# Causal attention with two routed expert layers on one core: score tiles paired 3 with 0 and 2 with 1, and another order of the products in odd and even steps

## The chip, the cores and the metric

The program runs on one NeuronCore of a Trainium2 chip. TensorE (PE in the profile, with its weight loads as PEld) multiplies matrices into PSUM, which has eight banks; VectorE (DVE) and ScalarE (ACT) read PSUM and work on SBUF; GpSimd (POOL) and SyncE (SP) issue transfers, and GpSimd does some elementwise work. The metric is the device time of one execution in microseconds, median of several runs.

## The reference, cut to what matters

```
attn (4 batches, 12 heads, 448 rows, 64 wide):
  scores = q @ k.T / 8, masked above the diagonal
  p = exp(scores - max(scores)); p = p / (sum(p) + 1e-9); x = p @ v
x -> 1792 tokens x 768
moe : skip = x @ w_skip; e = argmax(x @ w_gate); g = softmax at e
      where skip > 0:  x = x + g * (relu(x @ w1[e]) @ w2[e])
moe2: e = argmax(xn @ en.T / tau), xn and en with unit norm; g = softmax at e
      x = g * (relu(x @ w1[e]) @ w2[e])
```

## The kernel before

The first quarter of the program (up to 235 us) is attention and the first router; the rest sends tokens to 8 experts twice. The change is all in attention.

Attention is one loop over the 48 heads, `i` = 0 to 47. It runs under `manual_schedule`, so on each engine the instructions stand in the order in which the code emits them, and each engine takes them in that order; what one engine needs of another it waits for by semaphore. Step `i` works on several heads at once:

- scores of head `i-1`: the 448 rows are four chunks of 112, and by causality chunk `c` has (c+1)*112 columns. `scores` (L303) writes one product for each chunk, in the order 2, 3, 1, 0. q and k of a head are 64 deep and lie twice in SBUF, on partitions 0 to 63 and on 64 to 127, so that a product uses one half of the array's rows: `r` picks the half.
- `stage_a` (L310): for a chunk, one VectorE instruction scales, masks and takes the row maximum (L318, `st` and `mn`), and one ScalarE instruction takes exp and the row sum (L321, `pr`).
- `turn` (L550), head `i-2`: ten transposes of `pr` by TensorE in three groups (L331, tiles `tp`), each group copied to SBUF (L333, `pt`): the first and third by VectorE, the second by ScalarE.
- for pairs of heads: in an even step `stage_v` (L336) multiplies the turned weights by v for heads `i-4` and `i-3` (16 matmul rows of the trace, tile `av`), ScalarE copies it (L347, `xb`); in the odd step that follows, `turn_v` (L349) transposes `xb` (L353, `tv`), `norm_v` (L356) divides by the row sums on VectorE (L359 to L361, tile `x`), `put_x` sends x to DRAM, and `router_turn` (L370) transposes x (L373, `rt`), which ScalarE copies (L376, `xs`); in the next even step `router_pair` (L378) multiplies it by the router's weights (L386) and VectorE adds it up (L391, `ls`).
- when a batch of 12 heads is through, `route` (L401) hands single pieces to the following steps through the list `later`: `logits` (L393, in steps 17, 29 and 41), `rank` (L454, steps 19, 31 and 43; its sum `rks` L476), one-hot lists on GpSimd, and `enter` (L521, `tk`; steps 24, 27, 36 and 39).

In an odd step from 5 on TensorE has, in order: scores, ten transposes, the router's four transposes. In an even step: scores, values, router's products, ten transposes, and at its end the four transposes of `turn_v` for the odd step that follows. In the odd steps 7 to 17 ScalarE also casts 128x1024 of a later layer's weights (L637).

PSUM: tile `s3` has a bank; chunks 2 and 0 share the tile `s20` in one bank; chunk 1, the router's products `lt` and the logits share the tile `bank`; `tp`, `tv`, `rt`, `rk` and `tk` rotate through four banks; `av` has one. A reader or writer of a tile waits for the last other user of the whole tile, whichever columns it used.

Of the kernel before, what the change touches and what calls it, by code (L numbers as in the profile page):

```python
# [7 lines left out]
F32 = mybir.dt.float32  # L8
# [10 lines left out]
B, H, S, D = 4, 12, 448, 64  # L19
CP = 112  # L20
NCH = S // CP
DM = H * D
DF = 1024
NE = 8
# [21 lines left out]
def moe_attention_kernel(tc, qk, vv, w_r, emb, tau, w11, w12, w21, w22, out):  # L46
# [25 lines left out]
    with ExitStack() as top:  # L72
# [148 lines left out]
        with ExitStack() as ctx:  # L221
# [34 lines left out]
            ern, en = inv_norm(sm, ess, NE, "en")  # L256

            def embed_squares():
                esq = wk.tile([NE, DM], F32, tag="pt", name="esq")
                nc.scalar.activation(esq, es, AF.Square, accum_out=ess)  # L260

            def embed():
                pe = ps.tile([P, 4 * CP], F32, tag="tp", name="pe", bufs=4)
                for k in range(KC):
                    nc.tensor.transpose(
                        pe[:, k * 8 : k * 8 + 8], es[:, k * P : (k + 1) * P], ident[:NE, :NE])
                nc.vector.tensor_copy(wr[:, :, 8:16], pe[:, 0:48].rearrange("p (k e) -> p k e", e=8))
# [8 lines left out]
                    small.pop(0)()  # L276


            bank = ps.tile([P, 4 * P], F32, tag="s1", name="bank")
            lt, lg_room = bank[:, 2 * CP : 3 * CP], bank[:CP, 3 * CP : 3 * CP + NCH * NLG]  # L280

            def busy_here(n):
                if n:
# [10 lines left out]
            def score_tiles():  # L294
                return dict(
                    st=wk.tile([CP, 10 * CP], F32, tag="st", name="st"),
                    mn=wk.tile([CP, NCH], F32, tag="mn", name="mn"),
                    pr=wk.tile([CP, 10 * CP], F32, tag="pr", name="pr"),
                    s3=ps.tile([CP, S], F32, tag="s3", name="s3"),
                    s20=ps.tile([CP, S], F32, tag="s20", name="s20"),  # L300
                    s1=bank[:CP, 0 : 2 * CP])

            def scores(src, a, c):  # L303

                n, r = (c + 1) * CP, 64 * (1 - c % 2)
                a[c] = (a["s20"][:, 3 * CP :], a["s1"], a["s20"][:, 0 : 3 * CP], a["s3"])[c]
                nc.tensor.matmul(a[c], src[r : r + 64, c * CP : (c + 1) * CP], src[r : r + 64, S : S + n],  # L307
                                 start=True, stop=True)

# [14 lines left out]
            def turn_p(pr, pt, i):  # L324

                nb = 4 if i < 2 else 2
                tp = ps.tile([CP, 4 * CP], F32, tag="tp", name="tp", bufs=4)
                for u in range(nb):
                    c, j = BLOCKS[4 * i + u]
                    o = (OFF[c] + j) * CP  # L330
                    nc.tensor.transpose(tp[:, u * CP : (u + 1) * CP], pr[:, o : o + CP], ident[:CP, :CP])  # L331
                dst = pt[:, 4 * i * CP : (4 * i + nb) * CP]
                (nc.scalar.copy if i == 1 else nc.vector.tensor_copy)(dst, tp[:, : nb * CP])  # L333

            def stage_v(g):

                b, hp = divmod(g, H // 2)
                av = ps.tile([P, S], F32, tag="av", name="av")
                for j in range(NCH):
                    o = BLOCKS.index((j, j)) * CP  # L340
                    for u in range(2):
                        nc.tensor.matmul(av[u * D : (u + 1) * D, j * CP :], v_t[b][:, j, 2 * hp + u, :],  # L342
                                         pts[2 * g + u][:, o : o + (NCH - j) * CP],
                                         start=(j == 0), stop=(j == NCH - 1))
                del pts[2 * g], pts[2 * g + 1]
                xb = wk.tile([P, S], F32, tag="xb", name="xb", bufs=1)
                return lambda: nc.scalar.copy(xb, av), xb  # L347

            def turn_v(xb):  # L349

                tv = ps.tile([CP, NCH, P], F32, tag="tp", name="tv", bufs=4)
                for t in range(NCH):
                    nc.tensor.transpose(tv[:, t, :], xb[:, t * CP : (t + 1) * CP], ident)  # L353
                return tv

            def norm_v(g, tv):  # L356
                b, hp = divmod(g, H // 2)
                rs = sums.pop(g)
                nc.vector.tensor_scalar(rs, rs, 1e-9, None, op0=ALU.add)  # L359
                nc.vector.reciprocal(rs, rs)  # L360
                nc.vector.tensor_tensor(  # L361
                    x_t[b][:, :, hp * P : (hp + 1) * P].rearrange("p t (u d) -> p t u d", u=2),
                    tv.rearrange("p t (u d) -> p t u d", u=2),
                    rs.unsqueeze(3).to_broadcast([CP, NCH, 2, D]), op=ALU.mult)
# [2 lines left out]

                return b == B - 1 and k == KC - 1

            def router_turn(b, k):  # L370
                rt = ps.tile([P, 4 * CP], F32, tag="tp", name="rt", bufs=4)
                for t in range(NCH):
                    nc.tensor.transpose(  # L373
                        rt[:, t * CP : (t + 1) * CP], x_t[b][:, t, k * P : (k + 1) * P], ident[:CP, :CP])
                xs = wk.tile([P, S], F32, tag="xs", name="xs")
                return lambda: nc.scalar.copy(xs, rt), (b, k, xs)  # L376
# [24 lines left out]
            def route(b):  # L401
# [51 lines left out]

                def rank():  # L454
                    oh, some = k["oh"], k["some"]
                    rk = ps.tile([P, 4 * CP], F32, tag="tp", name="rk", bufs=4)
                    wd = NCH * 16
                    o16 = oh.rearrange("p t m e -> p t (m e)")
                    r16 = run[:CP].rearrange("p m e -> p (m e)")
# [60 lines left out]

                def enter(m):  # L521
                    roh, voh = k["made"][m]
                    tk = ps.tile([P, NCOL], F32, tag="tp", name="tk", bufs=4)
                    for t in range(NCH):
                        nc.tensor.matmul(tk, roh[:, t, :], voh[:, t, :], start=(t == 0), stop=(t == NCH - 1))
                    if fast:
                        first_index(0, tk)
                    nc.vector.tensor_tensor(tok[m], tok[m], tk, op=ALU.add)
                    while k["fill"]:
                        fill()  # L530
# [17 lines left out]
                        lambda: both(enters[0], q1), q2, q3, enters[1]]  # L548

            def turn(i):  # L550
                pts[i] = wk.tile([CP, 10 * CP], F32, tag="pt", name="pt")
                for u in range(3):
                    turn_p(prs[i], pts[i], u)

            def put_x(g):
                b, hp = divmod(g, H // 2)
                if hp % 2 == 1:
                    c0, c1 = (hp - 1) * P, (hp + 1) * P
                    for xx in (x1, x2):
                        xd = xx[b * S : (b + 1) * S, :].rearrange("(t p) f -> p t f", p=CP)  # L560
                        nc.sync.dma_start(xd[:, :, c0:c1], x_t[b][:, :, c0:c1])
# [11 lines left out]
            spl, prs, pts, sums = {}, {}, {}, {}  # L573
            with tc.manual_schedule():
                busy_here(12)
                exps = []
                for i in range(n):
                    b, h = heads[i]
                    if h == 0:
# [13 lines left out]
                        early_low(EARLY[i])  # L593
                    even = i % 2 == 0
                    if not even and i >= 5:
                        norm_v(i // 2 - 2, turn_v(xb))
                        put_x(i // 2 - 2)
                    if i >= 1:
                        sc = score_tiles()
                        prs[i - 1] = sc["pr"]  # L600
                        for c in (2, 3, 1, 0):
                            scores(spl[i - 1], sc, c)
                        exps = [stage_a(i - 1, sc, c) for c in (2, 3, 1)]
                        exps.pop(0)()
                        little()
                    little()
                    ended = None
                    if even and i >= 4:
                        copy_v, xb = stage_v(i // 2 - 2)
                    add = None  # L610
                    if even and i >= 6:
                        add = router_pair(*pair)
                        ended = pair[0] if pair[1] == KC - 1 else None
                    while exps:
                        exps.pop(0)()
                    if even and i >= 4:
                        copy_v()
                    if i >= 1:
                        stage_a(i - 1, sc, 0)()
                        little()  # L620
                    if add is not None:
                        add()
                    if i == 0:
                        embed_squares()
                    little()
# [5 lines left out]
                    if not even and i >= 5:  # L631
                        copy_x, pair = router_turn(*divmod(i // 2 - 2, H // 2))
                        copy_x()
                    if i == 3:
                        embed()
                    if i + 1 in EARLY:
# [16 lines left out]
                    exps.pop(0)()  # L653
                add()
                turn(n - 2)
                norm_v(n // 2 - 2, turn_v(xb))
                later.pop(0)()
                turn(n - 1)
                copy_x, pair = router_turn(B - 1, KC - 2)
                later.pop(0)()  # L660
                copy_x()
                copy_v, xb = stage_v(n // 2 - 1)
# [544 lines left out]
```

## Time and profile before

| | |
|---|---|
| median of 3 runs | 901.4 us (897.3 to 902.94) |
| profiled execution | 902.78 us, span of the trace 901.1 us |
| PE busy | 824.0 us (91%) |
| DVE, ACT, POOL busy | 554.4 (62%), 474.8 (53%), 135.2 us (15%) |
| mean granted TensorE clock | 0.978 of full speed |
| steps 45 and 46, one pair of heads | 8.39 us, PE 8.09 of it |

Times below are microseconds from the start of the span. A step is counted from the first score product on TensorE to the next step's. The trace groups matmuls of one line and tile that follow each other; a float32 product shows as two matmul rows (two passes).

### The profile page before, as it was taken

What the parts mean: (1) busy time and instruction counts of PE and PEld (TensorE: products, weight loads), DVE (VectorE), ACT (ScalarE), POOL (GpSimd) and SP (SyncE); (2) the same over time, 40 slices, a digit from 0 to 9 for tenths busy, and PEclk for the clock granted to TensorE, in tenths of its full rate; (3) what the DMA queues carried; (4) which work ended last, traced back from release to release, by engine and by line L of the source; (5) the groups of instructions that cost most, each with busy time, mean ns of one, the idle gap of its engine ahead of it and who ended that gap; (6) DMA issues with size and microseconds to landing.
All of it is one profiled execution on the core that took longest, in us unless ns stands there. A gap on an engine that the chain in (4) does not pass through costs nothing. (4 is left out here: it accounts for less than half of the span.)

```text
span 901.1 us, 14898 instructions
## 1 busy us (share of the span) xinstructions
PE 824.0 (91%) x4960; PEld 686.5 (76%) x4960; DVE 554.4 (62%) x1641; ACT 474.8 (53%) x1013; POOL 135.2 (15%) x150
## 2 busy tenths in 40 slices
PE   7998989989797899899999879899999998999994
PEld 5665766666487788788899748789889887889884
DVE  5767767776566688378833476665283268574343
ACT  5777666666455466166612336454272256463252
POOL 1132404013201111011010021011111011110100
PEclk9999999999899899999999999999999999999998
DMA  8979565563636487267710354580451086361000
GB/s 243 315 271 299 165 185 165 167 206 139 202 140 258 175 300 286 72 232 300 299 45 28 145 198 159 197 332 21 149 211 51 19 313 267 133 238 41 37 1 18
DMA packets 59032, 158.22 MB, mean 176 GB/s; under 512 B 13013, under 2 KB 23765, under 8 KB 58448
## 3 DMA queue, kind: packets, MB, share of 16 engines
q1 hardware_dynamic: 52816, 139.33, 43.4%
q0 software_dynamic: 6080, 17.29, 5.4%
q8 instruction: 59, 0.97, 0.5%
q14 instruction: 77, 0.63, 0.2%
HBM read 146.45 MB, written 22.92 MB: 188 GB/s over the span
## 5 line engine op out<-in xcount | busy, mean ns | idle before, releaser
L789 PE MATMUL p<-hi,ht 128*128 128x384 f32 x960 | 241.8, 353 | 8.5 <-DVE ht L773 4.6
L740 DVE TENSOR_TENSOR lo<-raw,hi 128x768 fp32r<-128x768 f32 (+1 forms) x218 | 220.6, 1062 | 8.0 <-ACT hi L736 4.5
L781 PE MATMUL p<-hi,xt 128*128 128x512 f32 x720 | 183.3, 403 | 8.0 <-PEq L1088 3.3
L736 ACT CAST hi<-raw 128x768 fp32r<-128x768 f32 (+1 forms) x218 | 187.3, 923 | 0.6 <-DMA raw<-in_w 0.6
L789 PEld LDWEIGHTS p<-hi,ht 128*128 128x128 f32 x960 | 167.8, 191 | 14.7 <-DVE ht L773 10.6
L781 PEld LDWEIGHTS p<-hi,xt 128*128 128x128 f32 x720 | 140.4, 198 | 37.4 <-ACTq L1088 5.1
L321 ACT ACTIVATE pr<-st,mn 112x336 f32<-112x336 f32 x192 | 99.5, 520 | 60.4 <-DVE mn L318 60.4
L789 PE MATMUL p<-lo,ht 128*128 128x384 f32 x480 | 124.3, 340 | 0.4 <-issue 0.4
L773 DVE SCALAR_TENSOR_TENSOR ht<-tp,ht 128x512 fp32r<-128x512 f32 x60 | 41.4, 689 | 115.3 <-ACT ht L772 106.6
L781 PE MATMUL p<-lo,xt 128*128 128x512 f32 x360 | 96.2, 402 | 0.0
L940 ACT COPY hs<-p 128x512 f32<-128x512 f32 x60 | 34.8, 580 | 106.0 <-PE p L781 67.0
L789 PEld LDWEIGHTS p<-lo,ht 128*128 128x128 f32 x480 | 88.7, 191 | 0.5 <-issue 0.5
L760 ACT CAST xt<-tp 128x384 fp32r<-128x384 f32 (+2 forms) x62 | 30.4, 492 | 109.5 <-PE tp L754 108.8
L761 DVE TENSOR_TENSOR xt<-tp,xt 128x384 fp32r<-128x384 f32 (+2 forms) x62 | 33.3, 544 | 84.5 <-ACT xt L760 81.6
L318 DVE CUSTOM_DVE_ANT_0 st<-s,mask 112x336 f32<-112x336 f32 x144 | 63.5, 465 | 29.4 <-PE s L307 17.8
L781 PEld LDWEIGHTS p<-lo,xt 128*128 128x128 f32 x360 | 67.8, 195 | 11.4
L772 ACT ACTIVATE ht<-tp 128x512 fp32r<-128x512 f32 x60 | 36.0, 600 | 55.1 <-PE tp L798 49.4
L331 PE MATMUL tp<-ident,pr 112*112 112x112 f32 x480 | 57.3, 267 | 0.0
L307 PE MATMUL s<-qk 64*112 64x112 f32 (+2 forms) x288 | 49.6, 450 | 7.1 <-DVE mn L318 7.1
L331 PEld LDWEIGHTS tp<-ident,pr 112*112 112x112 f32 x480 | 47.1, 136 | 8.6 <-issue 7.8
L818 POOL DMA_INDIRECT out<-py,pidx x18 | 19.7, 1093 | 207.7 <-ACT hi L736 75.5
L342 PE MATMUL av<-pt,v 112*64 112x448 f32 (+3 forms) x384 | 50.6, 405 | 0.0
(201 smaller groups left out, 908.3 us busy)
## 6 DMA issues: line engine op xcount, KB each, us to landing
raw<-in_w SPq DMA_DIRECT2D x96, 512.0 KB
raw<-in_w SPq DMA_DIRECT2D x128, 384.0 KB
qk<-in_qk SPq DMA_DIRECT2D x23, 896.0 KB
x<-x SPq DMA_DIRECT2D x24, 448.0 KB
v<-in_vv SPq DMA_DIRECT2D x4, 1344.0 KB
qk<-in_qk SPq DMA_DIRECT2D x2, 448.0 KB
g_n<-x,L POOLq DMA_INDIRECT x23, 4.4
out<-py,pidx POOLq DMA_INDIRECT x18, 3.4
```

Source lines behind the costliest of these rows:

```text
L307: nc.tensor.matmul(a[c], src[r : r + 64, c * CP : (c + 1) * CP], src[r : r + 64, S : S + n], start=True, stop=True)
L318: nc.vector.tensor_tensor_reduce(out=so, in0=a[c], in1=mask[:, S - n : S], scale=-0.125, scalar=3.0e38, op0=ALU.add, op1=ALU.min, accum_ou ...
L321: return lambda: nc.scalar.activation(a["pr"][:, OFF[c] * CP : OFF[c] * CP + n], so, AF.Exp, bias=mn, scale=-1.0, accum_out=rs)
L331: nc.tensor.transpose(tp[:, u * CP : (u + 1) * CP], pr[:, o : o + CP], ident[:CP, :CP])
L342: nc.tensor.matmul(av[u * D : (u + 1) * D, j * CP :], v_t[b][:, j, 2 * hp + u, :], pts[2 * g + u][:, o : o + (NCH - j) * CP], start=(j == ...
L736: copy(hi, raw)
L740: eng.tensor_tensor(lo, raw, hi.bitcast(F32), op=ALU.subtract)
L772: nc.scalar.activation(hi, src, AF.Relu)
L773: nc.vector.scalar_tensor_tensor(lo, src, 0.0, hi.bitcast(F32), op0=ALU.max, op1=ALU.subtract)
L781: nc.tensor.matmul(p1[u], xt[:, k, :, j], r[:, u * 512 : (u + 1) * 512], start=(k == 0 and j == 0 and not low), stop=(k == KC - 1 and low))
L789: mm = nc.tensor.matmul(p2[u], l, r[:, u * (DM // 2) : (u + 1) * (DM // 2)], start=(f == 0 and j == 0), stop=(f == FC - 1 and j == len(ter ...
L940: nc.scalar.copy(hs[:, u * 512 : (u + 1) * 512], p1[u])
```

## The change

- Score tiles: chunks 0 and 3 now take one half of the array's rows, 1 and 2 the other (before: 1 and 3, 0 and 2). Each of the four has a PSUM tile of its own; the router's products and the logits now share the tile `bank` with chunk 0.
- An odd step is now: VectorE's adding of the router's products and ScalarE's copy of the values first, then scores, maxima of chunks 2 and 3, `turn_v` and `norm_v`, maxima of chunks 1 and 0, `turn`, `router_turn`.
- An even step is now: scores, all four maxima, `turn`, then the router's products, and the values last.
- The rotating `tp` tiles are three instead of four; `tv` and `rt` share the bank of `av`; `pt` has three buffers.

```diff
-            bank = ps.tile([P, 4 * P], F32, tag="s1", name="bank")
-            lt, lg_room = bank[:, 2 * CP : 3 * CP], bank[:CP, 3 * CP : 3 * CP + NCH * NLG]
+            bank = ps.tile([P, 4 * P], F32, tag="s0", name="bank")
+            lt, lg_room = bank[:, CP : 2 * CP], bank[:CP, 2 * CP : 2 * CP + NCH * NLG]
...
-                n, r = (c + 1) * CP, 64 * (1 - c % 2)
-                a[c] = (a["s20"][:, 3 * CP :], a["s1"], a["s20"][:, 0 : 3 * CP], a["s3"])[c]
+                n, r = (c + 1) * CP, (0, 64, 64, 0)[c]
+                a[c] = (a["s0"], a["s1"], a["s2"], a["s3"])[c]
...
-                av = ps.tile([P, S], F32, tag="av", name="av")
+                av = turned_room("av")[:, 0:S]
...
+            def turned_room(tag):
+
+                return ps.tile([P, 4 * P], F32, tag=tag, name="turned", bufs=3 if tag == "tp" else 1)
+
+            def turn_v(xb, tag="av"):
+
+                tv = turned_room(tag)[:CP].rearrange("p (t n) -> p t n", t=NCH)
...
                     if not even and i >= 5:
-                        norm_v(i // 2 - 2, turn_v(xb))
-                        put_x(i // 2 - 2)
+                        copy_v()
+                        if add is not None:
+                            add()
                     if i >= 1:
...
-                        exps = [stage_a(i - 1, sc, c) for c in (2, 3, 1)]
-                        exps.pop(0)()
+                        exps = [stage_a(i - 1, sc, c) for c in (2, 3)]
                         little()
                     little()
-                    ended = None
-                    if even and i >= 4:
-                        copy_v, xb = stage_v(i // 2 - 2)
-                    add = None
-                    if even and i >= 6:
-                        add = router_pair(*pair)
-                        ended = pair[0] if pair[1] == KC - 1 else None
+                    if not even and i >= 5:
+                        norm_v(i // 2 - 2, turn_v(xb))
+                        put_x(i // 2 - 2)
+                    if i >= 1:
+                        exps += [stage_a(i - 1, sc, c) for c in (1, 0)]
                     while exps:
                         exps.pop(0)()
...
                     if not even and i >= 5:
                         copy_x, pair = router_turn(*divmod(i // 2 - 2, H // 2))
                         copy_x()
+                    ended, add = None, None
+                    if even and i >= 6:
+                        add = router_pair(*pair)
+                        ended = pair[0] if pair[1] == KC - 1 else None
+                    if even and i >= 4:
+                        copy_v, xb = stage_v(i // 2 - 2)
```

The order of instructions, first VectorE in an odd step (`rs` and `x` are `norm_v`, `s_…` and `bank` the score tiles; `pt` is a copy of `turn`). Before:

```order
L359 TENSOR_SCALAR rs<-rs 112x8
L360 RECIPROCAL rs<-rs 112x8 [waits DVE_49]
L361 TENSOR_TENSOR x_123<-tv,rs 112x4x128 [waits DVE_49,PE_49]
L318 ISA st,mn<-s_605,mask 112x336 [waits PE_49,Activation_49]
L318 ISA mn 112x1
L318 ISA st,mn<-s_604,mask 112x448
L318 ISA mn 112x1
L318 ISA st,mn<-bank,mask 112x224
L318 ISA mn 112x1
L318 ISA st,mn<-s_605,mask 112x112
L318 ISA mn 112x1
```

The same step of the changed kernel:

```order
L396 TENSOR_TENSOR ls<-ls,bank 128x112 [waits PE_49]
L319 ISA st,mn<-s_605,mask 112x336 [waits PE_49,Activation_49]
L319 ISA mn 112x1
L319 ISA st,mn<-s_604,mask 112x448 [waits PE_49]
L319 ISA mn 112x1
L364 TENSOR_SCALAR rs<-rs 112x8
L365 RECIPROCAL rs<-rs 112x8 [waits DVE_49]
L366 TENSOR_TENSOR x_123<-turned,rs 112x4x128 [waits DVE_49,PE_49]
L319 ISA st,mn<-s_606,mask 112x224
L319 ISA mn 112x1
L319 ISA st,mn<-bank,mask 112x112
L319 ISA mn 112x1
```

`norm_v` moved from ahead of the four maxima to between the second and the third, and the maxima of chunks 2 and 3 have each a wait of its own.

TensorE in the odd step of the changed kernel, with the four transposes of `turn_v` (L358) after the scores and the router's (L378) last, up to the scores of the even step; the wait of L378 is for `x`:

```order
L308 MATMUL s_605<-qk_435 112x336 [waits DMAHW5_49]
L308 MATMUL s_604<-qk_435 112x448
L308 MATMUL s_606<-qk_435 112x224
L308 MATMUL bank<-qk_435 112x112 [waits DVE_49]
L358 MATMUL turned<-ident,xb 112x128 [waits Activation_49]
L358 MATMUL turned<-ident,xb 112x128 x3
L332 MATMUL tp<-ident,pr 112x112 x10
L378 MATMUL turned<-ident,x_123 128x112 [waits DVE_49]
L378 MATMUL turned<-ident,x_123 128x112 x3
L308 MATMUL s_661<-qk_435 112x336
```

Before, L353 (`turn_v`) stood at the end of the even step, ahead of the odd step's scores, and the scores of the even step waited for VectorE.

TensorE in the even step, from the router's products on. Before:

```order
L386 MATMUL bank<-xs,wr 32x112 [waits DVE_49,Activation_49]
L386 MATMUL bank<-xs,wr 32x112 x3
L331 MATMUL tp<-ident,pr 112x112 [waits PE_49]
L331 MATMUL tp<-ident,pr 112x112 x3
L331 MATMUL tp<-ident,pr 112x112 [waits PE_49]
L331 MATMUL tp<-ident,pr 112x112 x5
L353 MATMUL tv<-ident,xb 112x128 [waits Activation_49]
L353 MATMUL tv<-ident,xb 112x128 x3
```

The changed kernel:

```order
L391 MATMUL bank<-xs,wr 32x112 [waits DVE_49,Activation_49]
L391 MATMUL bank<-xs,wr 32x112 x3
L343 MATMUL turned<-pt,v_121 64x448 [waits PE_49]
L343 MATMUL turned<-pt,v_121 64x448
L343 MATMUL turned<-pt,v_121 64x336 x2
L343 MATMUL turned<-pt,v_121 64x224 x2
L343 MATMUL turned<-pt,v_121 64x112 x2
```

The values (L342, now L343) moved from ahead of the router's products to behind them. In the changed kernel the wait of L391 for VectorE is for the maximum of chunk 0, which lies in the same tile; before, it was for that of chunk 1.

## Rows read from the trace of the kernel before

**Rows 1.** Steps 45 and 46 together: us, busy us of each engine.
```profile
sum 8.39, PE 8.09 PEld 5.71 DVE 6.12 ACT 6.11 POOL 6.58; mean PE 4.04 PEld 2.85 DVE 3.06 ACT 3.06 POOL 3.29
```

**Rows 2.** Timeline of TensorE, steps 45 and 46: start, us, line, out<-in.
```profile
203.81 1.01 PE L307 MATMUL s<-qk 64*112 64x336 f32 x6
...
206.99 1.01 PE L307 MATMUL s<-qk 64*112 64x336 f32 x6 [0.30 <-DVE mn L318]
207.84 0.54 PE L307 MATMUL bank<-qk 64*112 64x224 f32 x2
208.31 2.11 PE L342 MATMUL av<-pt,v 112*64 112x448 f32 x16
210.34 0.40 PE L386 MATMUL bank<-xs,wr 128*32 128x112 f32 x8
210.67 1.17 PE L331 MATMUL tp<-ident,pr 112*112 112x112 f32 x10
211.68 0.60 PE L353 MATMUL tv<-ident,xb 128*112 128x128 f32 x4
212.21 0.63 PE L307 MATMUL s<-qk 64*112 64x336 f32 x2
```

**Rows 3.** Timeline of VectorE, steps 45 and 46.
```profile
203.81 0.16 DVE L359 TENSOR_SCALAR rs<-rs 112x8 f32<-112x8 f32 x1
...
204.30 0.69 DVE L361 TENSOR_TENSOR x<-tv,rs 112x512 f32<-112x512 f32 x1
...
206.85 0.08 DVE L318 DVE_READ_ACCUMULATOR2_ANT mn<- 112x1 f32 x1
...
208.54 0.51 DVE L318 CUSTOM_DVE_ANT_0 st<-s,mask 112x336 f32<-112x336 f32 x1 [0.77 <-ACT pt L333]
...
208.97 0.62 DVE L318 CUSTOM_DVE_ANT_0 st<-s,mask 112x448 f32<-112x448 f32 x1
...
209.51 0.38 DVE L318 CUSTOM_DVE_ANT_0 st<-bank,mask 112x224 f32<-112x224 f32 x1
...
209.83 0.27 DVE L318 CUSTOM_DVE_ANT_0 st<-s,mask 112x112 f32<-112x112 f32 x1
210.02 0.08 DVE L318 DVE_READ_ACCUMULATOR2_ANT mn<- 112x1 f32 x1
```

**Rows 4.** Timeline of ScalarE, from step 45's third exp to its last copy.
```profile
207.14 0.46 ACT L321 ACTIVATE pr<-st,mn 112x224 f32<-112x224 f32 x1
...
208.39 0.52 ACT L376 COPY xs<-rt 128x448 f32<-128x448 f32 x1
```

**Rows 5.** Steps 12, 17, 19, 27, 29, 30, 41: us, busy us (instructions), granted clock, DMA.
```profile
50.58:56.19 5.61, 5.44 (x46) 3.47 (x47) 3.80 (x15) 5.61 (x19) 2.36 (x1) 1.00 0.93 271
73.76:78.42 4.66, 3.07 (x25) 2.44 (x24) 3.28 (x13) 2.73 (x10) 0.00 (x0) 1.00 1.05 357
83.64:87.82 4.18, 3.28 (x28) 2.50 (x27) 3.80 (x18) 2.19 (x10) 0.00 (x0) 1.00 1.01 366
118.41:122.29 3.88, 3.18 (x27) 2.40 (x26) 3.38 (x15) 1.84 (x8) 0.00 (x0) 1.00 0.48 131
127.52:132.88 5.36, 3.77 (x26) 3.00 (x25) 4.12 (x18) 2.75 (x10) 0.00 (x0) 0.86 0.87 245
132.88:139.04 6.16, 6.16 (x48) 4.15 (x47) 3.62 (x20) 3.72 (x12) 0.00 (x0) 0.84 0.43 150
182.91:189.00 6.09, 4.50 (x26) 3.73 (x25) 4.12 (x18) 3.03 (x10) 0.00 (x0) 0.75 0.23 87
```

**Rows 6.** Timeline of TensorE: start of step 2's scores, and of step 17's logits.
```profile
9.10 1.01 PE L307 MATMUL s<-qk 64*112 64x336 f32 x6 [2.04 <-DVE mn L318]
...
76.74 0.41 PE L396 MATMUL bank<-ident,ls 128*112 128x68 f32 x2 [1.59 <-DVE mn L318]
```

**Rows 7.** Timeline of VectorE, step 19: first and last instruction of the rank.
```profile
86.57 0.26 DVE L469 TENSOR_REDUCE some<-oh 112x16 bf16<-112x64 bf16 x1
...
87.02 0.22 DVE L476 COPY rks<-rk 112x64 f32<-112x64 f32 x1
```

More of the change, by code (lines that the diff above doesn't have):

```diff
@@ L258, in embed_squares @@
             def embed_squares():
-                esq = wk.tile([NE, DM], F32, tag="pt", name="esq")
+                esq = wk.tile([NE, DM], F32, tag="pt", name="esq", bufs=3)
                 nc.scalar.activation(esq, es, AF.Square, accum_out=ess)
             def embed():
-                pe = ps.tile([P, 4 * CP], F32, tag="tp", name="pe", bufs=4)
+                pe = ps.tile([P, 4 * CP], F32, tag="tp", name="pe", bufs=3)
                 for k in range(KC):
@@ L299, in score_tiles @@
                     s3=ps.tile([CP, S], F32, tag="s3", name="s3"),
-                    s20=ps.tile([CP, S], F32, tag="s20", name="s20"),
-                    s1=bank[:CP, 0 : 2 * CP])
+                    s2=ps.tile([CP, 3 * CP], F32, tag="s2", name="s2"),
+                    s1=ps.tile([CP, 2 * CP], F32, tag="s1", name="s1"),
+                    s0=bank[:CP, 0:CP])
             def scores(src, a, c):
-                n, r = (c + 1) * CP, 64 * (1 - c % 2)
-                a[c] = (a["s20"][:, 3 * CP :], a["s1"], a["s20"][:, 0 : 3 * CP], a["s3"])[c]
+                n, r = (c + 1) * CP, (0, 64, 64, 0)[c]
+                a[c] = (a["s0"], a["s1"], a["s2"], a["s3"])[c]
                 nc.tensor.matmul(a[c], src[r : r + 64, c * CP : (c + 1) * CP], src[r : r + 64, S : S + n],
@@ L326, in turn_p @@
                 nb = 4 if i < 2 else 2
-                tp = ps.tile([CP, 4 * CP], F32, tag="tp", name="tp", bufs=4)
+                tp = ps.tile([CP, 4 * CP], F32, tag="tp", name="tp", bufs=3)
                 for u in range(nb):
@@ L347, in stage_v @@
                 return lambda: nc.scalar.copy(xb, av), xb
-            def turn_v(xb):
-                tv = ps.tile([CP, NCH, P], F32, tag="tp", name="tv", bufs=4)
+            def turned_room(tag):
+                return ps.tile([P, 4 * P], F32, tag=tag, name="turned", bufs=3 if tag == "tp" else 1)
+            def turn_v(xb, tag="av"):
+                tv = turned_room(tag)[:CP].rearrange("p (t n) -> p t n", t=NCH)
                 for t in range(NCH):
@@ L368, in direct, with router_turn @@
                 return b == B - 1 and k == KC - 1
-            def router_turn(b, k):
-                rt = ps.tile([P, 4 * CP], F32, tag="tp", name="rt", bufs=4)
+            def router_turn(b, k, tag="av"):
+                rt = turned_room(tag)[:, 0 : 4 * CP]
                 for t in range(NCH):
@@ L455, in rank @@
                     oh, some = k["oh"], k["some"]
-                    rk = ps.tile([P, 4 * CP], F32, tag="tp", name="rk", bufs=4)
+                    rk = ps.tile([P, 4 * CP], F32, tag="tp", name="rk", bufs=3)
                     wd = NCH * 16
@@ L522, in enter @@
                     roh, voh = k["made"][m]
-                    tk = ps.tile([P, NCOL], F32, tag="tp", name="tk", bufs=4)
+                    tk = ps.tile([P, NCOL], F32, tag="tp", name="tk", bufs=3)
                     for t in range(NCH):
@@ L550, in turn @@
             def turn(i):
-                pts[i] = wk.tile([CP, 10 * CP], F32, tag="pt", name="pt")
+                pts[i] = wk.tile([CP, 10 * CP], F32, tag="pt", name="pt", bufs=3)
                 for u in range(3):
@@ L575, in moe_attention_kernel @@
                 busy_here(12)
-                exps = []
+                exps, add = [], None
                 for i in range(n):
@@ L602, in moe_attention_kernel @@
                             scores(spl[i - 1], sc, c)
-                        exps = [stage_a(i - 1, sc, c) for c in (2, 3, 1)]
-                        exps.pop(0)()
+                        exps = [stage_a(i - 1, sc, c) for c in (2, 3)]
                         little()
                     little()
-                    ended = None
-                    if even and i >= 4:
-                        copy_v, xb = stage_v(i // 2 - 2)
-                    add = None
-                    if even and i >= 6:
-                        add = router_pair(*pair)
-                        ended = pair[0] if pair[1] == KC - 1 else None
+                    if not even and i >= 5:
[3 more added lines that the diff above has]
+                        exps += [stage_a(i - 1, sc, c) for c in (1, 0)]
                     while exps:
                         exps.pop(0)()
-                    if even and i >= 4:
-                        copy_v()
                     if i >= 1:
-                        stage_a(i - 1, sc, 0)()
                         little()
-                    if add is not None:
-                        add()
                     if i == 0:
@@ L655, in moe_attention_kernel @@
                 turn(n - 2)
-                norm_v(n // 2 - 2, turn_v(xb))
+                norm_v(n // 2 - 2, turn_v(xb, "tp"))
                 later.pop(0)()
                 turn(n - 1)
-                copy_x, pair = router_turn(B - 1, KC - 2)
+                copy_x, pair = router_turn(B - 1, KC - 2, "tp")
                 later.pop(0)()
```

## The prediction, made before the changed kernel ran

> **What bounds the kernel now.** I read first what a pair of steps costs and who is busy in it, then TensorE's timeline of the pair, then VectorE's beside it. The pair of steps 45 and 46 takes 8.39 us and TensorE is busy for 8.09 of it, VectorE for 6.12 and ScalarE for 6.11 [rows 1]. So TensorE's own order sets the pace, with one wait in the pair: the scores of the even step wait for VectorE's last maximum, idle 0.30 [rows 2]. All of it repeats in 14 of the 22 odd steps from 5 on; the other eight carry the logits, the rank or the tokens of a finished batch and are longer [rows 5]. The experts behind attention are not touched, and they begin when the last batch is routed, so a shift of attention's end is a shift of the program's.
>
> **Prices on TensorE.** From one start to the next in the even step: scores 1.32 (206.99 to 208.31), values 2.03, router's products 0.33, ten transposes 1.01, four transposes of the values 0.53 [rows 2]; I price the router's four transposes at 0.53 too.
>
> **Halves of the array.** A score product is two passes, and the two halves run side by side. Before, the longer half has 2 x (448 + 224) = 1344 columns, after the change each has 2 x (448 + 112) = 1120. The price of a column: values are 2 x (448 + 336 + 224 + 112) = 2240 columns in 2.03, scores 1344 in 1.32, so 0.71 for 896 more, 0.8 ns each. The change saves 224 columns, 0.18 a step; scores become 1.14. If TensorE alone set the pace, the 0.18 in each of 47 steps would be 8.5 us, and the wait of 0.30 plus what surrounds it would go as well.
>
> **When the first maximum can start.** Before, VectorE starts the first maximum at 208.54, 1.55 after the scores, 0.16 after the last score product has ended (207.84 + 0.54 = 208.38) [rows 2, 3]. With tiles of their own chunk 2 is released alone: its two passes are 672 columns instead of 1344, so it ends at 1.39 - 0.54 = 0.85, and with the same 0.16 the first maximum starts 1.01 after the scores. Chunk 3 comes in meanwhile. From one to the next on VectorE: chunk 2 0.43, chunk 3 0.54, chunk 1 0.32, chunk 0 0.19 and 0.08 for its read [rows 3].
>
> In an even step every score product now raises the semaphore for itself, where before one did. The Trainium skill (TensorE: Matmul & The Clock Gate, Part 3, "The cost: per-tile semaphore tail") puts 26.3 ns on each such increment, since they are served one after the other. By that, an estimate from the page, three more in 21 even steps and one more in 22 odd ones, all on the path, would add 2.2 us; the 0.16 above, measured with one increment, does not show it.
>
> **Odd step.** The chain that now decides it: scores, maxima of chunks 2 and 3, then `norm_v`, then the router's transposes, which need `x`. Maximum 2 starts at 1.01, maximum 3 at 1.44, `norm_v` at 1.98; its first instruction to `x` is 0.49, `x` takes 0.69 [rows 3]: `x` is ready at 3.16. TensorE restarts 0.06 after VectorE's end (206.85 + 0.08 to 206.99) [rows 2, 3], at 3.22; with 0.53 for the transposes the next scores start at 3.75. TensorE's own work up to there is 1.14 + 0.53 + 1.01 = 2.68, so it idles 0.54 in front of the router's transposes; before, `norm_v` ran under the scores and nothing waited for it. The step was 3.18 (203.81 to 206.99): **+0.57**. The copy of the values now precedes the exps on ScalarE; it starts as the values end and has 1.14 of scores for its cover. `put_x` stands behind the later `x` on SyncE, and behind it the next pair's q and k; they are used two steps on, so I cost this at nothing.
>
> **Even step.** Scores 1.14, transposes to 2.15, then the router's products, which wait for the maximum of chunk 0, since its tile is theirs too: 1.01 + 0.43 + 0.54 + 0.32 + 0.19 + 0.08 + 0.06 = 2.63. TensorE idles 0.48, and the values are queued behind. Then 0.33 and 2.03: 4.99, against 5.22 (206.99 to 212.21): **-0.23**. The four transposes of the values have left this step, which is why it is still shorter. The products need ScalarE's `xs` as well: the third exp of the odd step starts when maximum 1 is read, at 3.16 + 0.32 + 0.08 = 3.56, and from its start to the end of `xs` are 1.77 (207.14 to 208.91) [rows 4], so 5.33; the products want it at 3.75 + 2.63 = 6.38. Not the bound.
>
> A pair is thus 8.74 instead of 8.40, **+0.34**, with TensorE idle for 1.0 of it instead of 0.3.
>
> **Counting.** Profiled execution, attention:
> - 14 ordinary odd steps at +0.57: +8.0.
> - 14 ordinary even steps at -0.23: -3.2. Five more (8 to 16) took 5.61 before, with ScalarE busy all the time for its cast [rows 5]; ScalarE is not in the new chain, so -0.62 each: -3.1. Steps 24 and 36, with tokens, at nothing.
> - Three odd steps with logits: the logits wait for the maximum of chunk 0, as they did for chunk 1's (1.59 [rows 6]), but this now comes after `x`: 3.16 + 0.32 + 0.19 + 0.08 + 0.06 = 3.81; from the logits to the next scores are 1.68 (76.74 to 78.42) [rows 5, 6]: 5.49 against 4.66, +2.5 in all.
> - Three with the rank: maximum 0 starts at 3.48, the rank's first instruction 0.19 later, and its sum is read 0.67 after that (86.57 to 87.24) [rows 7], at 4.34. With three `tp` tiles the third group of transposes waits for it, where before only the router's did: 4.34 + 0.06 + 0.20 + 0.53 = 5.13 against 4.18: +2.9. Two with tokens, whose adding is as wide as chunk 0 (0.27): 3.67 + 0.27 + 0.06 + 0.20 + 0.53 = 4.73 against 3.88: +1.7.
> - Start: step 2's scores waited 2.04 for all of step 1's maxima [rows 6], now for chunk 2's alone. Between nothing (exps and loads are late next) and -2.0; I take -1.0.
> - End: behind the loop the values wait in the shared bank for `xs`, and tokens for one of three tiles; 0 to +1.0 by the 0.5 each that these waits were above; I take +0.8.
>
> Sum **+8.5**.
>
> **The clock.** The granted clock fell to 1.2 GHz around the logits of steps 29 and 41 (0.86 and 0.75 in these stretches) and not of step 17 (1.00), after the same idle stretch of TensorE, 1.59 (4.66 less 3.07 busy) [rows 5]. One fall cost (5.36 - 4.66) + (6.16 - 5.22) = 1.64. Now TensorE idles from 1.67 to 3.81, 2.1, at the logits, and at the rank from 2.7 to 4.4, 1.7, where it idled 0.9. Six stretches longer than the one that cost the clock twice in three: between none and four falls more, none to +6.6; I take two, **+3.3**.
>
> Together +11.8: 914.6 by the profiled 902.78, which lies 1.4 above the median. On the median of 901.4 it is 913; I predict **912.5**.
>
> **Rivals.** *TensorE still sets the pace.* Its own work in the pair is 1.14 + 0.53 + 1.01 + 0.53 and 1.14 + 1.01 + 0.33 + 2.03 = 7.72, 0.68 less than before. This decides if `x` is ready by 2.68 instead of 3.16 and maximum 0 by 2.15 instead of 2.63, that is if VectorE starts half a microsecond earlier than I have it. Then 21 pairs save 14, the five cast steps 1.9 more, and the special steps lose little: 886. Against it speaks that the first product of a step cannot end before 0.85. In the Trainium skill (TensorEngine Tiling (Array Packing), "PSUM Bottleneck") tiling speeds up TensorE but not the reading of PSUM; by that rule the saved columns are not had. VectorE's 6.12 of 8.39 alone would not show it. Chance 0.05.
>
> *The chain is as I say but shorter, and the clock does not fall more.* Were the 0.16 only the 0.06 seen between VectorE and TensorE, twice in 21 pairs, that is 4.2 less; with the start at -2.0 and no further fall, 901.4 + 8.5 - 4.2 - 1.0 = 905, within 1%. Chance 0.33.
>
> *The halves do not run side by side as counted,* so that scores keep 1.32. The chains go through chunk 2's end and VectorE, with 0.5 of idle TensorE behind, so the time stays 912; only the trace would tell. It is in the forecast's chance, 0.62.
>
> **How the numbers follow.** 1% of this kernel, 9 us, is about what a measurement can tell from no change; the bounds are 892.4 and 910.4. Low end: the shorter chain, the start and one fall fewer than before, 903. High end: four falls more than before, start and end at their worst, 901.4 + 8.5 + 6.6 + 1.2, and 1.4 for the spread of the runs, 919. Faster 0.06, within 1% 0.36, slower 0.58.
>
> **What would show it.** Right: odd steps of 3.7 with TensorE waiting some 0.5 for `x` ahead of L378; even steps of 5.0 with a wait for `mn` ahead of L391; logits steps of 5.4; more falls of the clock in attention. Scores of 1.14 show the halves. Wrong: pairs under 8.4, or a first maximum that starts well before 1.0; or even steps in which ScalarE's `xs` comes last.

## The result, and the profile after

The changed kernel takes 909.8 us (median of 4 runs, 908.07 to 910.38) against 901.4: ratio 1.008, 95% interval 1.0053 to 1.0108. It is slower by 0.8%, forecast 912.5 in a range of 903 to 919. The profiled execution took 909.96 us, its span 908.3, 7.2 more than before.

First steps 45 and 46 as a whole, which answer to [rows 1]: us, then busy us of each engine, granted clock, DMA.

```profile
211.53:220.37 8.84, 7.95 (x70) 5.77 (x69) 6.03 (x24) 6.19 (x20) 6.59 (x11) 1.00 0.58 229
```

The pair is 0.44 longer, 8.84 instead of 8.40, while TensorE has less to do in it than before and is idle for 0.9 instead of 0.3. TensorE's timeline of the pair, with start, us, line and tile, shows where (compare [rows 2]):

```profile
211.53 1.19 PE L308 MATMUL s<-qk 64*112 64x336 f32 x6
212.38 0.35 PE L308 MATMUL bank<-qk 64*112 64x112 f32 x2
212.67 0.65 PE L358 MATMUL turned<-ident,xb 128*112 128x128 f32 x4
213.15 1.12 PE L332 MATMUL tp<-ident,pr 112*112 112x112 f32 x10
214.80 0.60 PE L378 MATMUL turned<-ident,x 112*128 112x112 f32 x4 [0.52 <-DVE x L366]
215.33 1.19 PE L308 MATMUL s<-qk 64*112 64x336 f32 x6
216.18 0.35 PE L308 MATMUL bank<-qk 64*112 64x112 f32 x2
216.46 1.17 PE L332 MATMUL tp<-ident,pr 112*112 112x112 f32 x10
218.00 0.40 PE L391 MATMUL bank<-xs,wr 128*32 128x112 f32 x8 [0.37 <-DVE mn L319]
218.33 2.11 PE L343 MATMUL turned<-pt,v 112*64 112x448 f32 x16
220.37 0.63 PE L308 MATMUL s<-qk 64*112 64x336 f32 x2
```

Read it from wait to wait. The scores last 1.14 (211.53 to 212.67) instead of 1.32: the halves gave the 0.18. But the router's transposes stand 0.52 waiting for `x`, and the router's products 0.37 for a maximum, each with everything behind it in the queue. The old wait of 0.30 ahead of the scores is gone.

VectorE in the same odd step (compare [rows 3]) is the one waited for:

```profile
212.50 0.51 DVE L319 CUSTOM_DVE_ANT_0 st<-s,mask 112x336 f32<-112x336 f32 x1 [2.46 <-PE s L308]
...
212.93 0.62 DVE L319 CUSTOM_DVE_ANT_0 st<-s,mask 112x448 f32<-112x448 f32 x1
...
213.47 0.25 DVE L364 TENSOR_SCALAR rs<-rs 112x8 f32<-112x8 f32 x1
...
214.05 0.69 DVE L366 TENSOR_TENSOR x<-turned,rs 112x512 f32<-112x512 f32 x1
214.66 0.38 DVE L319 CUSTOM_DVE_ANT_0 st<-s,mask 112x224 f32<-112x224 f32 x1
...
216.29 0.51 DVE L319 CUSTOM_DVE_ANT_0 st<-s,mask 112x336 f32<-112x336 f32 x1 [0.22 <-PE s L308]
```

The first maximum starts 0.97 after the scores in the odd step (212.50 less 211.53) and 0.96 in the even one (1.01 predicted), `x` is done at 214.74, and its reader on TensorE starts 0.06 later.

The steps with more in them, by the same windows as [rows 5]: step 4, logits steps 17 and 29, rank step 19, token step 27, logits step 41 and the even step 42.

```profile
16.23:22.07 5.84, 5.84 (x36) 3.92 (x34) 2.79 (x11) 2.68 (x9) 0.00 (x0) 0.71 0.78 285
74.65:81.45 6.80, 4.90 (x30) 4.13 (x29) 4.03 (x17) 3.33 (x10) 0.00 (x0) 0.78 1.05 320
86.68:91.56 4.88, 3.53 (x33) 2.93 (x31) 4.04 (x18) 3.21 (x10) 0.00 (x0) 1.00 0.82 300
123.41:128.01 4.60, 3.47 (x32) 2.86 (x31) 3.50 (x14) 2.97 (x10) 0.00 (x0) 1.00 0.13 37
133.05:138.42 5.37, 3.47 (x31) 2.85 (x29) 3.62 (x14) 3.27 (x10) 0.00 (x0) 1.00 1.02 262
189.84:195.82 5.98, 4.08 (x30) 3.32 (x28) 4.03 (x17) 3.33 (x10) 0.00 (x0) 0.89 0.30 119
195.82:201.51 5.69, 5.69 (x44) 3.77 (x43) 3.64 (x20) 3.23 (x11) 0.00 (x0) 0.82 0.40 135
```

The column after the engines is the granted clock. Step 29 had full speed, 2.4 GHz, and shows what logits now cost: 5.37 against 5.49 predicted. Steps 4, 17, 41 and 42 hold stretches at 1.2 GHz, from three falls. Ahead of each TensorE had stood still: in step 3 for the copies of the turn, in steps 17 and 41 for the maximum of chunk 0 (1.90 both times; compare [rows 6]). The same 1.90 in step 29 brought no fall. The third row is the rank's wait, 1.35, after which the clock stayed at 1.00:

```profile
15.77 0.53 PE L265 MATMUL pe<-ident,x 8*128 8x8 f32 x6 [2.07 <-DVE pt L334]
...
78.34 0.57 PE L401 MATMUL bank<-ident,ls 128*112 128x68 f32 x2 [1.90 <-DVE mn L319]
...
90.84 0.41 PE L332 MATMUL tp<-ident,pr 112*112 112x112 f32 x2 [1.35 <-DVE rks L481]
```

Put together, from the starts of the steps in both traces, up to the last logits of attention (225.52 before, 235.15 after):

| | predicted | traced |
|---|---|---|
| 14 ordinary odd steps | +8.0 | +8.0 (44.4 to 52.4) |
| 11 ordinary even steps and the 5 with casts | -5.6 (11 x -0.23, 5 x -0.62) | -4.8 (-1.95, -2.85) |
| 3 logits steps and the even step after each | +1.8 (+2.5, 3 x -0.23) | +1.2, two clock falls in either kernel |
| 3 rank steps | +2.9 | +2.1 |
| 4 token steps | +1.7 | +1.6 |
| first four steps, and their start | -1.0 | +0.6, with one clock fall |
| end | +0.8 | +0.9 |
| further clock falls | +3.3 (two) | the one in the line of the first four steps |
| sum | +11.8 | +9.6 |

Behind that point the work is the same, and took 2.4 less in this execution (673.1 against 675.6), so that the span grew by 7.2. The medians differ by 8.4.

### The profile page after: what moved, and what is told of

Read it like the earlier page. It is cut to its first block, busy times and chain, and to the rows that moved or that the text cites. A ratio compares the mean times of both kernels' runs of the same rounds, so it can differ in the third digit from the quotient of the medians.

```text
span 908.3 us, 14815 instructions
## 1 busy us (share of the span) xinstructions
PE 818.2 (90%) x4960; PEld 686.6 (76%) x4960; DVE 552.2 (61%) x1641; ACT 477.8 (53%) x1013; POOL 138.4 (15%) x150
## 5 line engine op out<-in xcount | busy, mean ns | idle before, releaser
L319 DVE CUSTOM_DVE_ANT_0 st<-s,mask 112x336 f32<-112x336 f32 x144 | 67.2, 503 | 59.9 <-PE s L308 59.8
L308 PE MATMUL s<-qk 64*112 64x224 f32 (+2 forms) x288 | 59.7, 486 | 0.3 <-DVE mn L319 0.3
L343 PE MATMUL turned<-pt,v 112*64 112x448 f32 (+3 forms) x384 | 50.9, 407 | 0.4 <-ACT xs L381 0.4
```

Source lines behind the costliest of these rows:

```text
L319: nc.vector.tensor_tensor_reduce(out=so, in0=a[c], in1=mask[:, S - n : S], scale=-0.125, scalar=3.0e38, op0=ALU.add, op1=ALU.min, accum_ou ...
```

## The experiments

Eight kernels, all built from the changed one. Each was timed beside the kernel before, whose median was 901.95 with old_halves, products_room, norm_last and turn_next and 901.77 with the other four; small differences between kernels are better read from the ratios. The pair is steps 45 and 46 of the one execution of each that was traced.

| kernel | pair, us | median, us | ratio to before, 95% interval |
|---|---|---|---|
| changed | 8.84 | 909.8 | 1.008 [1.0053, 1.0108] |
| old_halves | 8.84 | 909.2 | 1.0065 [1.004, 1.009] |
| products_room | 8.31 | 902.8 | 1.0014 [0.999, 1.0039] |
| norm_last | 9.30 | 912.6 | 1.012 [1.0089, 1.015] |
| turn_alone | 8.53 | 904.1 | 1.0025 [1.0007, 1.0042] |
| logits_embed_room | 8.81 | 900.4 | 0.9984 [0.9966, 1.0002] |
| turn_next | 7.66 | 889.8 | 0.9868 [0.9846, 0.9891] |
| next_old_halves | 8.04 | 893.4 | 0.9921 [0.9897, 0.9945] |
| next_embed_room | 7.67 | 886.4 | 0.9828 [0.9806, 0.985] |

The theory is the prediction's: a chain through VectorE sets both steps, by way of `x` in the odd and of the maximum of chunk 0 in the even one. The main rival is its first rival, that TensorE's own work still sets the pace.

**old_halves: are the columns that the halves save worth anything here?**

```diff
-                n, r = (c + 1) * CP, (0, 64, 64, 0)[c]
+                n, r = (c + 1) * CP, 64 * (1 - c % 2)
```

> The changed kernel with the old assignment of chunks to halves of the rows (1 and 3, 0 and 2), nothing else undone. Theory (VectorE's chain sets both steps, TensorE idles 0.52 us ahead of the router's transposes and 0.37 us ahead of the router's products): score products get 0.18 us longer per step, the idle time shrinks by as much, odd steps stay at 3.73 and even steps at 5.04, the time stays at 910. Rival (TensorE's own work sets the pace): 47 steps by 0.18 us, 8.5 us more, 918.

Measured 909.2, and a pair as long as that of the changed kernel, with scores of 1.32 again (219.33 to 220.65). The two waits in TensorE's timeline of that pair:

```profile
222.59 0.60 PE L378 MATMUL turned<-ident,x 112*128 112x112 f32 x4 [0.33 <-DVE x L366]
...
225.80 0.40 PE L391 MATMUL bank<-xs,wr 128*32 128x112 f32 x8 [0.19 <-DVE mn L319]
```

Both waits are shorter by just the 0.18 or 0.19 that the scores are longer (0.52 to 0.33, 0.37 to 0.19). That is how cover looks in a trace: the work grows, the wait behind it shrinks, the step stays. In the changed kernel the halves buy nothing; the rival falls. The execution traced was the slowest of six, 916.75, in part by falls of the clock in steps 4, 18, 29 and 42; the steps compared here ran at full speed.

**products_room: the even step's wait.** The router's products move to the bank of chunk 2, whose maximum is read first; the order of the instructions stays.

```diff
-            lt, lg_room = bank[:, CP : 2 * CP], bank[:CP, 2 * CP : 2 * CP + NCH * NLG]
+            lg_room = bank[:CP, 2 * CP : 2 * CP + NCH * NLG]
+            bank2 = ps.tile([P, 4 * P], F32, tag="s2", name="bank2")
+            lt = bank2[:, 3 * CP : 4 * CP]
...
-                    s2=ps.tile([CP, 3 * CP], F32, tag="s2", name="s2"),
+                    s2=bank2[:CP, 0 : 3 * CP],
```

> The changed kernel with the router's products in the bank of chunk 2 instead of chunk 0's, so that they wait for the maximum of chunk 2 and no longer for that of chunk 0. Theory: the idle 0.37 us ahead of the products goes, even steps 4.67 us, 19 to 22 of them, odd steps unchanged at 3.73: 7 to 8 us less than the changed kernel, 902. Rival (the products wait for ScalarE's xs, or the values behind them for something else that is as late): even steps stay at 5.04, time 910.

Measured 902.8, 7.0 under the changed kernel by the medians and 6.0 by the ratios. The transposes and the products on TensorE, even step:

```profile
207.42 1.17 PE L334 MATMUL tp<-ident,pr 112*112 112x112 f32 x10
208.52 0.40 PE L393 MATMUL bank<-xs,wr 128*32 128x112 f32 x8
208.85 2.11 PE L345 MATMUL turned<-pt,v 112*64 112x448 f32 x16
```

No bracket, so no wait: the products follow the transposes, and ordinary even steps are 4.60 (expected 4.67). In this order of the instructions the wait came from the tile that the products share.

**norm_last: the odd step's wait, made longer.** The division goes behind all four maxima.

```diff
-                    if not even and i >= 5:
-                        norm_v(i // 2 - 2, turn_v(xb))
-                        put_x(i // 2 - 2)
                     if i >= 1:
                         exps += [stage_a(i - 1, sc, c) for c in (1, 0)]
+                    if not even and i >= 5:
+                        norm_v(i // 2 - 2, turn_v(xb))
+                        put_x(i // 2 - 2)
```

> The changed kernel with the division by the row sums behind all four maxima of the odd step instead of between the second and the third. Theory (the odd step ends x plus the router's transposes): x comes later by the two maxima that now precede it, 0.50 us, so 14 ordinary odd steps go from 3.73 to 4.23, +7; the three logits steps lose their wait for the maximum of chunk 0 and gain up to 1.1 us each, -3; together 913 to 914. Rival (the odd step is held by the late exps of chunks 1 and 0, which now come 1.2 us earlier, or by VectorE's total work): odd steps 3.73 or less, 910 or less.

Measured 912.6. Ordinary odd steps are 4.23, and the router's transposes wait for `x` 0.46 longer; the logits, on the other hand, wait 0.80 instead of 1.90:

```profile
80.26 0.41 PE L401 MATMUL bank<-ident,ls 128*112 128x68 f32 x2 [0.80 <-DVE mn L319]
...
215.42 0.60 PE L378 MATMUL turned<-ident,x 112*128 112x112 f32 x4 [0.98 <-DVE x L366]
```

So `x` is what ends the odd step, and not the exps: that of chunk 1 starts 2.74 after the step here, and 3.55 in the changed kernel. The medians alone, 2.8 apart, would say little; the steps say it.

**turn_alone: the odd step's wait, taken away by itself.** The router's transposes stand behind the scores of the next even step, when `x` is long there.

```diff
                             scores(spl[i - 1], sc, c)
+                        if even and i >= 6:
+                            copy_x, pair = router_turn(*divmod(i // 2 - 3, H // 2))
+                            copy_x()
...
-                    if not even and i >= 5:
-                        copy_x, pair = router_turn(*divmod(i // 2 - 2, H // 2))
-                        copy_x()
```

> The changed kernel with only the router's transposes moved behind the scores of the next even step; division and products' bank as in the changed kernel. Theory (two waits, on one chain of VectorE): TensorE no longer waits for x and the odd step falls to 2.67, but VectorE is not done any earlier; its copies of the turn end at 4.5 us after the odd step's start, so the even step's maxima start 1.8 us into it instead of 0.96, and the wait of the router's products for the maximum of chunk 0 grows by most of what was won: even steps 5.7 to 5.9, pair 8.4 to 8.5, 902 to 905. Rival (the two waits are separate prices): even step stays at 5.04 plus nothing, pair 8.25, 899.

Measured 904.1, within what the theory gave and 5 above the rival. TensorE's timeline of the even step, from its scores to its products:

```profile
209.74 1.34 PE L308 MATMUL s<-qk 64*112 64x336 f32 x5
...
211.20 0.60 PE L378 MATMUL turned<-ident,x 112*128 112x112 f32 x4
211.64 1.14 PE L332 MATMUL tp<-ident,pr 112*112 112x112 f32 x10
213.22 0.40 PE L391 MATMUL bank<-xs,wr 128*32 128x112 f32 x8 [0.44 <-DVE mn L319]
```

And VectorE's first maximum of that step:

```profile
211.52 0.50 DVE L319 CUSTOM_DVE_ANT_0 st<-s,mask 112x336 f32<-112x336 f32 x1
```

The odd step is 2.67, the wait of 0.52 and the transposes have left it. But the even step's maxima now start 1.78 into it (211.52 less 209.74) with no wait in front, since VectorE had not done with the odd step. Its scores take 1.46 (209.74 to 211.20) instead of 1.14, as the tiles of chunks 1 and 0 are still being read, and the products wait 0.44 instead of 0.37. Of the 0.52 the pair keeps 0.31 (8.84 to 8.53). The theory had the place of the loss only half right: it expected most of it in the products' wait.

**turn_next: both waits taken away.** The edits of products_room, turn_alone and norm_last together; `x` is now wanted so late that the division may stand last.

> The changed kernel with both waits taken away: the router's transposes of an odd step stand behind the scores of the next even step, the router's products lie in chunk 2's bank, and the division stands behind the four maxima, as x is now wanted only at about 3.8 us. Theory: TensorE's own work is left, odd step 1.14 + 0.53 + 1.01 = 2.68, even step 1.14 + 0.53 + 1.01 + 0.33 + 2.03 = 5.04, pair 7.72 instead of 8.77; 19 pairs save 20 us, the steps with logits, rank and tokens a little: 888 to 892, faster than the kernel before as well. Rival (the halves were not worth what was counted, or ScalarE and VectorE, 6.1 us of work each in a pair, or the three tp tiles bind next): pair 8.2 to 8.4, 900 to 903.

Measured 889.8. An ordinary pair on TensorE has no wait left, as its even step shows (`bank` in the first row is the bank of chunk 2, which now holds the products too), and under it the whole pair:

```profile
193.74 0.53 PE L310 MATMUL bank<-qk 64*112 64x336 f32 x1
...
194.87 0.60 PE L380 MATMUL turned<-ident,x 112*128 112x112 f32 x4
195.31 1.12 PE L334 MATMUL tp<-ident,pr 112*112 112x112 f32 x10
196.37 0.40 PE L393 MATMUL bank<-xs,wr 128*32 128x112 f32 x8
196.70 2.11 PE L345 MATMUL turned<-pt,v 112*64 112x448 f32 x16
```

```profile
191.07:198.73 7.66, 7.66 (x70) 5.74 (x68) 5.85 (x24) 6.14 (x20) 7.16 (x11) 1.00 0.80 303
```

TensorE is busy for 7.66 of 7.66. This is the pair of 7.72 that the prediction worked out for "TensorE still sets the pace", reached by another order. Not every step gained: 24 and 36, with the tokens, went from 5.47 to 6.21.

**next_old_halves: the halves again, where TensorE paces.** turn_next with the edit of old_halves.

> The kernel turn_next with the old assignment of chunks to halves of the rows. Theory: there TensorE paces every step, so the 224 columns that the halves save are now worth their 0.18 us in each of 47 steps less what other waits hide in the special ones: 4 to 8.5 us more than turn_next, 894 to 898, odd steps 2.85. Rival (the halves do not run side by side as counted, and the price of a column is not had): 890, odd steps 2.67.

Measured 893.4: 3.6 above turn_next by the medians, just under the 4 that was the low end, and 4.8 by the ratios. From step 5 to 47 its trace is 4.4 longer, odd steps 2.86 against 2.67; its step 4 had no fall of the clock, which turn_next's had. The same edit is worth nothing in one order and some 4 us in another.

**logits_embed_room and next_embed_room: the clock.** The changed kernel with the logits in the bank of chunk 2 and step 3's transposes of the embedding (L265) in the bank of the values; and turn_next with the latter alone.

```diff
-                pe = ps.tile([P, 4 * CP], F32, tag="tp", name="pe", bufs=3)
+                pe = ps.tile([P, 4 * P], F32, tag="av", name="pe", bufs=1)
...
-            lt, lg_room = bank[:, CP : 2 * CP], bank[:CP, 2 * CP : 2 * CP + NCH * NLG]
+            lt = bank[:, CP : 2 * CP]
+            bank2 = ps.tile([P, 4 * P], F32, tag="s2", name="bank2")
+            lg_room = bank2[:CP, 3 * CP : 3 * CP + NCH * NLG]
```

> The changed kernel with the logits in the bank of chunk 2 (they then wait for its maximum and not for chunk 0's) and the transposes of the embedding, in step 3, in the bank of the values instead of a tp tile. Theory on the clock (it falls after TensorE's longest idle stretches in attention, 1.9 us at the logits and 2.1 us in step 3): both stretches go, no fall of the granted clock up to step 48, logits steps about 3.75 instead of 5.37, step 3 about 4; 4.9 for the logits, 1 for step 3 and 1.6 for each of three falls, 899. Rival (the falls come whatever the idle time): two to four falls in attention remain, 903 to 904.

> The kernel turn_next with the transposes of the embedding in the bank of the values. Theory: step 3 loses an idle stretch of 1.7 us, and with it the fall of the clock in step 4 goes: 1 + 1.6 us less, 887. Rival (the fall comes all the same): 889.

Measured 900.4 and 886.4. The windows of steps 3, 4 and 17 of logits_embed_room:

```profile
71.80:75.63 3.83, 3.51 (x31) 2.84 (x29) 2.73 (x13) 2.21 (x6) 0.00 (x0) 1.00 1.02 392
11.38:14.95 3.57, 2.81 (x26) 2.30 (x25) 3.50 (x19) 2.93 (x12) 0.00 (x0) 1.00 1.06 195
14.95:19.22 4.27, 4.27 (x36) 2.90 (x35) 3.63 (x18) 3.77 (x14) 0.00 (x0) 1.00 0.95 321
```

Step 4 is 4.27 at full clock where it was 5.84 at 0.71, so this fall cost 1.57. Falls are not all alike: in old_halves step 4 stood at 0.56 and took 7.72, 3.26 more than the 4.46 of next_old_halves at full clock:

```profile
16.23:23.95 7.72, 7.72 (x36) 4.51 (x34) 2.88 (x11) 2.68 (x9) 0.00 (x0) 0.56 0.66 243
```

The logits steps of logits_embed_room are 3.83, but the even step after each is 5.66 instead of 5.04, which the expectation had not counted. With the logits no longer waited for, the next step begins while VectorE is still choosing experts, its first maximum starts 1.59 after the scores (133.04 less 131.45, step 30), and the router's products wait:

```profile
133.04 0.50 DVE L321 CUSTOM_DVE_ANT_0 st<-bank,mask 112x336 f32<-112x336 f32 x1
...
134.74 0.40 PE L393 MATMUL bank<-xs,wr 128*32 128x112 f32 x8 [0.98 <-DVE bm L452]
```

Up to step 48 the granted clock stays at 1.00 in both kernels; for next_embed_room as one window from the first scores to the start of step 48:

```profile
5.80:198.12 192.32, 179.71 (x1572) 133.03 (x1572) 146.44 (x643) 146.40 (x469) 45.65 (x54) 1.00 0.78 242
```

Over the traces of all ten kernels, the fall in step 4 came in the six in which TensorE had waited 1.70 to 2.07 in step 3 and in none of the four with 0.63 to 1.51; around the logits it came 10 times of 15 in the five kernels with waits of 1.59 to 1.91 there, and never in 15 where they were 0.80 or less. The rank's 1.35 never brought one. These are counts from one execution of each kernel.

Not tried: the new halves in the order of before. With every chunk in a bank of its own that order has only three rotating tiles left, and with fewer banks two chunks of different halves would be written into one bank. The Trainium skill (TensorEngine Tiling (Array Packing), "Gotcha 1: PSUM Pressure") says that different row tiles cannot access the same bank at the same time, and no run here shows it. What the halves alone are worth in the old order stays open.

## Why the prediction was right

- *Odd step.* Predicted 3.75 with 0.54 of waiting for `x`; traced 3.73, in three of 14 some 3.80, with 0.44 to 0.55 of waiting. norm_last and turn_alone move it with `x`, as the chain says. Right.
- *Even step.* Predicted 4.99 with 0.48 of waiting for the maximum of chunk 0; traced 5.04 and 0.37. products_room takes the wait away by changing the bank alone. Right; ScalarE's `xs` was ready at 216.87, well ahead of 218.00, as its row shows (compare [rows 4]):

```profile
216.34 0.53 ACT L381 COPY xs<-turned 128x448 f32<-128x448 f32 x1
```

- *Halves.* Predicted 0.18 a step, hidden; 0.18 traced, and hidden (old_halves). The Trainium skill (TensorEngine Tiling (Array Packing), "PSUM Bottleneck") says that tiling speeds up TensorE and not the reading of PSUM. That the saved columns are then not had, as the prediction concluded, holds for the changed kernel and not for turn_next, where TensorE is busy 7.66 of 7.66 and the readers are no longer on the path.
- *Increments.* The four in the even step left no mark: its first maximum starts 0.96 after the scores, the odd step's 0.97. The 2.2 us that the prediction estimated from the 26.3 ns an increment of the Trainium skill (TensorE: Matmul & The Clock Gate, Part 3, "The cost: per-tile semaphore tail") are not seen. The first maximum waits only for chunk 2's increment, and the second follows it without a gap (212.93), so what the later increments take would be covered here; the 26.3 ns themselves no run measures.
- *Logits, rank, tokens, end.* Each within 0.3 us of its step: 5.37 for 5.49, 4.88 for 5.13, 4.60 for 4.73, and +0.9 for +0.8 at the end. Two at nothing, steps 24 and 36, cost 0.08 each.
- *Start.* Without the fall in step 4 the first four steps would have been 1.3 shorter (start of step 1 to start of step 5: 16.14 less 1.57, against 15.90), near the 1.0 taken. That is partly luck, as the 1.0 was the middle of a range: step 1 was 1.60 shorter, step 3 was 1.02 longer by the embedding's wait, which the prediction did not have, and the scores began 0.38 later.
- *The clock* is the term that was mis-sized. Two further falls at +3.3 were counted, from six waits at logits (2.1 by the prediction, 1.90 traced) and rank (1.7, traced 1.35, which is less than the 1.59 that the logits waited before). There was one, and it was at neither: the logits had two falls in either kernel, the rank had none, and the new one came in step 4, where the third `tp` tile made the embedding wait 2.07. The logits' longer wait (1.90 for 1.59) did not bring more of them. Without this term the sum, +8.5, is what the medians show, +8.4, but some of that agreement is chance: in the one execution traced attention grew by 9.6, one fall (1.57) included, and the part behind it took 2.4 less. The clock falls in that part too, at places that differ from trace to trace; TensorE was busy there for 614.6 us against 617.8, in as many products, which fits less time at 1.2 GHz, but how much of the 2.4 that makes stays open.
- *The chances.* Slower by more than 1%, above 910.4, had 0.58. The median, 909.8, lies just under that bound, in "within 1%", which had 0.36: the range and the mechanism held, the class thought likeliest did not come.

The rivals: TensorE did not set the pace (886 was reached only by another order). "Shorter chain and no more falls", 905, took 0.06 from the end of chunk 2's product to the first maximum; traced are 0.15, from 216.14, where the first passes of the scores end in this row (chunk 2's second is the last of them), to 216.29:

```profile
215.33 0.81 PE L308 MATMUL s<-qk 64*112 64x336 f32 x3
```

The chain was thus hardly shorter than forecast, and a fall did come. The third rival falls too: the scores took 1.14 and not 1.32, so the halves run side by side.

## What to carry to other kernels

An edit that makes an engine's work shorter is worth nothing until the engine is what the step waits for: the same halves gave 0 us in the changed kernel and 4 us in turn_next. Before an order is changed, follow each moved product to what it reads and to the tile that it shares: here one product stood behind an `x` that VectorE made late, another behind a maximum in a borrowed bank, and moving one (with the division, which could then stand last) and giving the other another bank turned 909.8 into 889.8 us. A wait that is taken out of a chain by itself comes back in part further down, since the engine that was waited for is no earlier (turn_alone kept 0.31 of 0.52).

## What the runs showed of the hardware that was not expected

The clock's falls in attention came only after TensorE's longer pauses, and the edits that took these out were followed by none: up to step 48 there is no fall in the two kernels whose waits at the logits and in step 3 are all 0.80 or less, nor in next_old_halves, which waited 1.51 in step 3. A longer pause did not always bring one (10 of 15 at the logits). The fall in step 4 of the changed kernel cost 1.57 us, that in old_halves twice as much. Taking out both the two waits of the pair and the embedding's pause gives the fastest version, next_embed_room, 886.4 us, 1.7% under the kernel before (ratio 0.9828, 0.9806 to 0.985).
